# Windowed attention and multiplicative FFN on one core: Q and K of the first batch loaded in thirds, w1 and w2 in quarters, two row blocks of w3 by SP in fp32, and a new order of the opening

## The chip, the core and the metric

The kernel runs on one core of a Trainium2 chip. The core has five engines with a queue each, worked off in order: PE (TensorE, matmuls), DVE (VectorE), ACT (ScalarE), POOL (GpSimd) and SP (SyncE), which here only issues transfers. 16 DMA engines move the data; POOL and SP (and once ACT) issue the transfers. The time is device microseconds (us) of one execution; lower is better.

## The reference

```python
# q, k, v: (8, 8, 576, 64) fp32 (batch, head, position, dim)
scores = (q @ k.T) / 8            # kept where 0 <= row - col < 64, else -1e9
attn   = softmax(scores)
x      = (attn @ v) as (8*576, 512) rows    # heads side by side
h      = ((x @ w1) * (x @ w2)) @ w3         # w1, w2: 512x1024, w3: 1024x1024
out    = h @ w_out                          # w_out: 1024x512, out (4608, 512) fp32
```

## The kernel before, in words

Everything is computed in fp16 with fp32 sums. Because nothing stands between w3 and w_out, the kernel first folds them on the chip into one matrix `wc_sb` = w3 @ w_out (1024x512). After that each token costs only x @ w1, x @ w2, the product, and one matmul by `wc_sb`.

The work has four kinds, and all of them meet on PE.

- **Fold.** w3 is cut into eight row blocks of 128 rows. `fold_t(fc)` (L469) transposes one block on PE by eight matmuls with the identity `ident16`, and copies the result from PSUM (the accumulators that PE writes) to the tile `w3Ts[fc]` (L476). `fold_mm(fc, c0, c1, cp)` (L478) multiplies it by columns c0 to c1 of w_out and copies the result into `wc_sb` with the engine `cp`.
- **Attention.** A batch has three groups of 192 query rows. `scores(n)` (L272) is 32 small matmuls on group n and leaves two halves, one for each two pairs of heads; `weigh(d)` (L296) takes half d: exp on ACT (L303), then the window mask, either by POOL with `affine_select` (L258, L260) or by DVE as a product with a ready band of ones (L308). `values(d)` multiplies the weights by V and ones (L337 for batches 0 to 2, L353 after), so that the sums of the softmax come out of the same matmuls; then log and exp on ACT (L343, L344) and a product on DVE (L345) give the columns of `xT`, the FFN's input. `transposes(b, which, hh)` (L219) turns loaded Q or K rows by DVE (L225), which `scores` needs. `copy_v` copies halves of V blocks on DVE.
- **FFN.** Tokens go in nine groups of 512. `ffn_ab(g, fc, nf, lo, hi)` (L401) makes nf blocks of 128 of the 1024 hidden columns for tokens lo to hi of group g: matmuls (L417), a copy by ACT (L422), a product by DVE (L423). `ffn_o(g, t)` (L426) multiplies 128 tokens by `wc_sb` (L435) and copies the result out (L437); `store` (L440) sends it away on SP's queue.
- **Filler.** `keep_busy(n)` (L502) is n matmuls of the identity by itself, whose result nobody reads.

PSUM has two pools: `ps_a`, two tiles used by `scores` and `values`, and `ps_f`, four tiles used in turn by the fold, the FFN and the filler. A matmul that needs the next tile of a pool waits until the copy that read its earlier contents is done.

The order of the work on each engine is the order of the calls in the source (L516 on): nothing is reordered. Loads are issued by POOL, with a cast from fp32 to fp16 on the way. At most eight of POOL's loads are outstanding: each takes one of eight semaphores in turn, and waits until the load that had it eight issues ago has landed. `load_qk` (L202) loads Q or K of a batch in four loads by head pairs; `load_w12` (L454) loads halves of w1 or w2, `load_wo` (L459) halves of w_out, `load_w3` (L463) two row blocks of w3. From `tick(24)` (L614) on the order comes from a loop that interleaves attention `tick`s with FFN parts by due times (L622 to L649).

In the opening, POOL first issues the four K loads of batch 0, then makes the identity, issues the four Q loads, half of w_out and two blocks of w3; PE runs 120 filler matmuls, `scores(0)`, 30 more, and then the fold begins. The FFN of group 0 (L575) starts when the fold and all of batch 0's attention are done.

Of the kernel before, what the change touches and what calls it, by code (L numbers as in the profile page):

```python
# [144 lines left out]
def kernel(  # L145
# [25 lines left out]
    EARLY = 2  # L171
# [28 lines left out]
    RUN = [9] * 3 + [2] * (B - 3)  # L200

    def load_qk(b, which, *hhs):  # L202
        src = k if which == "k" else q
        r = RUN[b]
        if (which, b) not in t16s:
            t16s[which, b] = sb.tile([P, 2, TI * D], FP16, name=which + "16", bufs=2)
        t = t16s[which, b]
        if not hhs:
            for j in range(NJ):
                nc.gpsimd.dma_start(  # L210
                    out=t[32 * j:32 * j + 32].rearrange("p hh (i n) -> p (hh i) n", n=r * D),
                    in_=src[b, 2 * j:2 * j + 2].rearrange("hh (i p r) d -> p (hh i) (r d)", p=32, r=r))
        for hh in hhs:
            for i in range(2):
                nc.gpsimd.dma_start(
                    out=t[:, hh, i * r * D:(i + 1) * r * D],
                    in_=src[b, hh:H:2, i * 32 * r:(i + 1) * 32 * r].rearrange("j (p r) d -> j p (r d)", p=32, r=r))

    def transposes(b, which, hh):  # L219

        dst = kTs if which == "k" else qTs
        r = RUN[b]
        if hh == 0:
            dst[b] = sb.tile([P, 2, S, 2], FP16, name=which + "T")
        nc.vector.transpose(  # L225
            dst[b][:, hh].rearrange("q t c -> q (t c)").bitcast(I32).rearrange("q (i p r) -> q i r p", p=32, r=r),
            t16s[which, b][:, hh].bitcast(I32).rearrange("p (i r e) -> p i r e", r=r, e=32))
# [44 lines left out]
    def scores(n, now=True):  # L272
# [19 lines left out]
        weigh(2 * n)  # L292
        if now:
            weigh(2 * n + 1)

    def weigh(d):  # L296
# [9 lines left out]
        if d % 2 == 1 and d < 6 * EARLY:  # L306
# [7 lines left out]
    def values(d):  # L314
# [11 lines left out]
        r = sb.tile([P, 2, 192], FP32, name="r")
        x0 = (b * S + q_base) % RING
        xs = xT[:, j0:j0 + 2, x0:x0 + 192]
        if b < SHORT:
# [15 lines left out]
            nc.vector.tensor_tensor(xs, o, r, ALU.mult)  # L345
            return
        for jj in range(2):
            first = True
            for a in range(2):
# [104 lines left out]
    def load_w12(i, half):  # L454
        cols = slice(half * 512, half * 512 + 512)
# [3 lines left out]
    def load_wo(half):  # L459
        cols = slice(half * 256, half * 256 + 256)  # L460
        nc.gpsimd.dma_start(out=wo16[:, :, cols], in_=moe_w_out[:, cols].rearrange("(e p) m -> p e m", p=P))  # L461

    def load_w3(n):  # L463
        fc = 2 * n
        dst = w3a[:, 2 * fc:2 * fc + 4, :].rearrange("p (f a) n -> p f (a n)", f=2) if n < 2 else \
            xT[:, fc - 4:fc - 2, 2 * S:2 * S + DF]
        nc.gpsimd.dma_start(out=dst, in_=moe_w3[fc * P:fc * P + 2 * P].rearrange("(f p) n -> p f n", p=P))

    def fold_t(fc):  # L469
# [6 lines left out]
        dve_cp(w3Ts[fc], tp)  # L476
# [39 lines left out]
    load_qk(0, "k")  # L516
# [170 lines left out]
```

## Time and profile before

| what | value |
|---|---|
| median of 3 runs | 268.73 us (267.65 to 269.23) |
| profiled execution | 268.59 us, of which 266.8 us span from first to last instruction and 1.79 us around it |
| granted TensorE clock | 0.997 |
| busy ACT / DVE / POOL | 151.4 / 169.7 / 178.7 us |
| bytes: POOL's queue / hardware queues of SP and ACT | 19.41 MB / 9.59 MB |

PE's timeline by stage, from the windows view (stretch, PE busy, PE idle):

| stretch (us) | what PE does | PE busy | idle |
|---|---|---|---|
| 0 to 17.4 | filler, scores(0), waiting for loads | 11.44 | 5.96 |
| 17.4 to 40 | fold, scores(1), scores(2), values(0) to values(5) | 22.20 | 0.40 |
| 40 to 54 | ffn_ab of group 0 | 14.00 | 0 |
| 54 to 73 | batch 1's attention, ffn_o of group 0, start of group 1 | 18.04 | 0.96 |
| 73 to 250 | the loop | 177.00 | 0 |
| 250 to 267 | last FFN parts, last stores | 11.71 | 5.29 |

A line of the timeline gives the start, the time from the first start to the last end, engine, code line, operation, what it writes and reads, the number of instructions, and in brackets how long the engine was idle before and for what. "Busy" on PE counts pipelined matmuls from start to modelled end. DMA rows give the destination and source tile; sizes of POOL's loads are those written (fp16).

### The profile page before, as it was taken

The numbers are of one execution on the slowest core, as the hardware profiler recorded it, in microseconds if no ns is written. First come the engines' busy times: TensorE is split into PE (matmuls) and PEld (weight loads), VectorE is DVE, ScalarE is ACT, GpSimd is POOL, SyncE is SP. The second block draws the span as 40 slices with busy tenths as digits, with TensorE's granted clock in tenths as the row PEclk, the third lists the DMA queues.
The fourth block names the chain that finished last, engine by engine and source line by source line (L and its number), as shares of the span: only waits on it lengthen the run. The fifth ranks groups of instructions, "written<-read, shape, count | busy, mean of one in ns | idle before, by whom it ended". The sixth has DMA issues, their size and how long they took to land.

```text
span 266.8 us, 6600 instructions
## 1 busy us (share of the span) xinstructions
PE 254.4 (95%) x2608; PEld 149.7 (56%) x2608; DVE 169.7 (64%) x260; ACT 151.4 (57%) x261; POOL 178.7 (67%) x243
## 2 busy tenths in 40 slices
PE   3979999998999999999999999999999999999992
PEld 3968654445886445545556984545455445444441
DVE  6644454978775675986687567668786565564531
ACT  1037474367656577758874855777498748342300
POOL 7979826679879999999898739687766345005000
PEclk9999999999999999999999999999999999999998
DMA  5999999999999999899999765998540040012013
GB/s 81 170 207 186 189 207 201 131 181 138 149 106 62 131 206 77 61 165 162 62 106 180 102 43 64 202 105 57 99 96 4 7 150 6 0 53 108 0 57 109
DMA packets 75380, 29.45 MB, mean 110 GB/s; under 512 B 62369, under 2 KB 69793, under 8 KB 75345
## 3 DMA queue, kind: packets, MB, share of 16 engines
q0 software_dynamic: 69920, 19.41, 74.9%
q1 hardware_dynamic: 5280, 9.46, 10.0%
q8 instruction: 21, 0.34, 0.6%
q14 instruction: 15, 0.11, 0.2%
q10 hardware_dynamic: 144, 0.13, 0.1%
HBM read 38.80 MB, written 9.44 MB: 181 GB/s over the span
## 4 chain that ended last, share of the span: by engine, by line
PE 87%; DMA 4%; POOL 2%; DVE 2%; ACT 2%; issue 1%; POOLq 0%; DVEq 0%
PE f_ps L417 48%; PE f_ps L435 22%; PE a_ps L353 5%; PE a_ps L286 4%; PE f_ps L481 4%; DMA ab<-in_moe_w_dram 4%; PE a_ps L337 3%; ACT pt L303 1%; PE f_ps L474 1%; POOL q L210 1%; POOL k L210 1%; DVE xT L345 1%; DVE kT L225 1%; POOL ab L461 0%; DVE pt L308 0%
## 5 line engine op out<-in xcount | busy, mean ns | idle before, releaser
L417 PE MATMUL f_ps<-xT,w_sb 128*128 128x512 f16 (+1 forms) x704 | 131.5, 341 | 0.0
L417 PEld LDWEIGHTS <-w_sb 128*128 128x128 f16 x704 | 66.3, 98 | 50.7 <-issue 0.2
L423 DVE TENSOR_TENSOR ab<-f_ps,a_sb 128x512 f16<-128x512 f32 x72 | 49.6, 689 | 33.0 <-PE f_ps L417 31.2
L303 ACT ACTIVATE pt<-a_ps 128x1024 f16<-128x1024 f32 (+1 forms) x48 | 44.5, 953 | 45.4 <-PE a_ps L286 45.4
L258 POOL TENSOR_SCALAR_AFFINE_SELECT pt<-pt 128x1024 f16<-128x1024 f16 (+2 forms) x56 | 46.1, 824 | 30.6 <-ACT pt L303 30.5
L435 PE MATMUL f_ps<-wc_sb,ab 128*128 128x512 f16 (+1 forms) x296 | 66.4, 374 | 0.0
L422 ACT COPY a_sb<-f_ps 128x512 f32<-128x512 f32 x72 | 41.8, 581 | 36.9 <-PE f_ps L417 36.4
L260 POOL TENSOR_SCALAR_AFFINE_SELECT pt<-pt 128x1024 f16<-128x1024 f16 (+2 forms) x56 | 46.5, 831 | 3.9
L435 PEld LDWEIGHTS <-ab 128*128 128x128 f16 x296 | 27.3, 98 | 28.8
L238 POOL DMA_DIRECT2D v<-in_v_dram x40 | 34.0, 860 | 1.0 <-issue 0.4
L362 DVE TENSOR_TENSOR xT<-a_ps,r 64x384 f16<-64x384 f32 x30 | 16.5, 550 | 22.0 <-ACT r L361 22.0
L437 DVE COPY t2k<-f_ps 128x512 f32<-128x512 f32 (+1 forms) x35 | 23.7, 679 | 8.4 <-PE f_ps L435 7.9
L210 POOL DMA_DIRECT2D q<-in_q_dram x32 | 19.7, 621 | 11.8 <-DMA w_sb<-in_moe_w_dram 8.3
L210 POOL DMA_DIRECT2D k<-in_k_dram x32 | 20.1, 634 | 1.6 <-POOLq L671 1.0
L353 PEld LDWEIGHTS <-v 128*128 128x128 f16 x240 | 15.1, 98 | 6.4
L345 DVE TENSOR_TENSOR xT<-a_ps,r 128x384 f16<-128x384 f32 x18 | 10.0, 553 | 13.0 <-ACT r L344 13.0
L359 ACT ACTIVATE ln_s<-a_ps 64x384 f32<-64x384 f32 x30 | 14.6, 487 | 5.8 <-PE a_ps L353 5.0
L353 PE MATMUL a_ps<-pt,v 128*128 128x128 f16 x240 | 17.2, 215 | 0.0
L363 DVE TENSOR_TENSOR xT<-a_ps,r 64x384 f16<-64x384 f32 x30 | 16.8, 561 | 0.4
L286 PEld LDWEIGHTS <-kT 32*128 32x128 f16 x768 | 10.9, 92 | 9.6 <-issue 9.3
L361 ACT ACTIVATE r<-ln_s 128x384 f32<-128x384 f32 x30 | 15.7, 523 | 1.0
L225 DVE STREAM_TRANSPOSE qT<-q 128x576 int32<-128x576 int32 x16 | 14.7, 928 | 1.6 <-DMA q<-in_q_dram 1.6
(44 smaller groups left out, 184.9 us busy)
## 6 DMA issues: line engine op xcount, KB each, us to landing
out_dram<-t2k SPq DMA_DIRECT2D x35, 256.0 KB
k<-in_k_dram POOLq DMA_DIRECT2D x32, 144.0 KB, 6.3
q<-in_q_dram POOLq DMA_DIRECT2D x32, 144.0 KB, 5.8
v<-in_v_dram POOLq DMA_DIRECT2D x32, 128.0 KB, 5.0
w_sb<-in_moe_w_dram POOLq DMA_DIRECT2D x4, 512.0 KB, 9.7
ab<-in_moe_w_out_dram POOLq DMA_DIRECT2D x2, 512.0 KB, 9.5
ab<-in_moe_w_dram POOLq DMA_DIRECT2D x2, 512.0 KB, 9.4
xT<-in_moe_w_dram POOLq DMA_DIRECT2D x2, 512.0 KB, 10.4
```

Source lines behind the costliest of these rows:

```text
L210: nc.gpsimd.dma_start(out=t[32 * j:32 * j + 32].rearrange("p hh (i n) -> p (hh i) n", n=r * D), in_=src[b, 2 * j:2 * j + 2].rearrange("hh ...
L238: nc.gpsimd.dma_start(out=vh[lo:P, c], in_=v[b, :, s0:s0 + P - lo, :].rearrange("h s d -> s h d"))
L258: nc.gpsimd.affine_select(out=sl, in_=sl, pattern=pat, compare_op=ALU.is_ge, fill=0.0, base=off, channel_multiplier=-1)
L260: nc.gpsimd.affine_select(out=sl, in_=sl, pattern=[[-s, m] for s, m in pat], compare_op=ALU.is_ge, fill=0.0, base=63 - off, channel_multip ...
L286: nc.tensor.matmul(s_ps[j // 2][:, j % 2, o0:o0 + m], kT[part, a, k0:k0 + P, c], qT[part, a, q0:q0 + m, c], start=(c == 0), stop=(c == 1), ...
L303: nc.scalar.activation(pt[:, :, :, 0:w], s_ps, AF.Exp, bias=-SHIFT, scale=scale)
L353: nc.tensor.matmul(o_ps[:, jj, o0:o0 + n], v16[:, si * 2 + bi, j0 + jj, a * D:a * D + P], pt[:, jj, a, c0:c0 + n], start=first, stop=(bi = ...
L417: nc.tensor.matmul(d[:, f * n + c0:f * n + c1], w[:, dc, (fc + f) * P:(fc + f + 1) * P], xT[:, dc, xc:xc + c1 - c0], start=first, stop=(dc ...
L422: act_cp(a_sb[:, 0:nf * n], a_ps[:, 0:nf * n])
L423: nc.vector.tensor_tensor(ab[:, fc:fc + nf, lo:hi], b_ps[:, 0:nf * n].rearrange("p (f n) -> p f n", f=nf), a_sb[:, 0:nf * n].rearrange("p ...
L435: nc.tensor.matmul(o_ps[:, 0:c1 - c0], ab[:, fc, t * P:t * P + P], wc_sb[:, fc, c0:c1], start=(fc == 0), stop=(fc == 7))
L437: cp(o_sb[:, c0:c1], o_ps[:, 0:c1 - c0])
```

## The change

The loads of batch 0's Q and K become twelve: for K and Q, for the even and the odd heads (hh), for each third i of the positions (192 rows, 96 KB in fp16); `transposes` gets a form for one third. w1 and w2 come in quarters of 256 columns. Row blocks 0 and 1 of w3 are loaded by SP as they are, 512 KB of fp32 each, into the space of `w2_sb` (which w2's loads fill later), and cast to fp16 in halves of 512 columns by ACT (block 0) and DVE (block 1). `scores` no longer calls `weigh`, and `values` is split into its matmuls and `norm` (log, exp, product), so that each can be placed by itself; which engine masks is given at each call. The order of the calls from the start to the first `ffn_ab` of group 1 is new. After `tick(24)` nothing changes. The diff, cut to its core:

```diff
-    RUN = [9] * 3 + [2] * (B - 3)
+    RUN = [6] + [9] * 2 + [2] * (B - 3)
...
+    def third(b, which, hh, i):
+        r = RUN[b]
+        src = k if which == "k" else q
+        return src[b, hh:H:2, i * 32 * r:(i + 1) * 32 * r].rearrange("j (p r) d -> j p (r d)", p=32, r=r)
+
+    def load_rows(fc, queue):
+        queue.dma_start(out=w2_sb.rearrange("p a n -> p (a n)").bitcast(FP32)[:, fc * DF:fc * DF + DF],
+                        in_=moe_w3[fc * P:fc * P + P])
+
+    def cast_rows(fc, x, cp):
+        n = DF // 2
+        cp(w3a[:, 2 * fc + x, :],
+           w2_sb.rearrange("p a n -> p (a n)").bitcast(FP32)[:, fc * DF + x * n:fc * DF + x * n + n])
+
...
+    def load_third(b, which, hh, i):
+        n = RUN[b] * D
+        nc.gpsimd.dma_start(out=t16_of(b, which)[:, hh, i * n:(i + 1) * n], in_=third(b, which, hh, i))
+
+    def transposes(b, which, hh, *i):
...
+        part = slice(i[0], i[0] + 1) if i else slice(0, TI // r)
         nc.vector.transpose(
-            dst[b][:, hh].rearrange("q t c -> q (t c)").bitcast(I32).rearrange("q (i p r) -> q i r p", p=32, r=r),
-            t16s[which, b][:, hh].bitcast(I32).rearrange("p (i r e) -> p i r e", r=r, e=32))
+            dst[b][:, hh].rearrange("q t c -> q (t c)").bitcast(I32).rearrange("q (i p r) -> q i r p", p=32, r=r)[:, part],
+            t16s[which, b][:, hh].bitcast(I32).rearrange("p (i r e) -> p i r e", r=r, e=32)[:, part])
 
...
-    def scores(n, now=True):
+    def scores(n):
...
-        weigh(2 * n)
-        if now:
-            weigh(2 * n + 1)
-
-    def weigh(d):
+
+    def weigh(d, engine=nc.gpsimd):
...
-        if d % 2 == 1 and d < 6 * EARLY:
+        if engine is nc.vector:
...
-            o, total = (o_ps[:, e, 0:384].rearrange("p (j n) -> p j n", j=2) for e in range(2))
-            nc.scalar.activation(y, total, AF.Ln)
-            nc.scalar.activation(r, y, AF.Exp, scale=-1.0)
-            nc.vector.tensor_tensor(xs, o, r, ALU.mult)
...
+    def norm(d):
+        b, r = divmod(d, 6)
...
+        if b < SHORT:
+            o, total = (o_ps[:, e, 0:384].rearrange("p (j n) -> p j n", j=2) for e in range(2))
+            nc.scalar.activation(y, total, AF.Ln)
+            nc.scalar.activation(r, y, AF.Exp, scale=-1.0)
+            nc.vector.tensor_tensor(xs, o, r, ALU.mult)
...
-    def load_w12(i, half):
+    def load_w12(i, c0, c1):
...
-    def fold_t(fc):
+    def fold_t(fc, cp):
...
-        dve_cp(w3Ts[fc], tp)
+        cp(w3Ts[fc], tp)
...
-    load_qk(0, "k")
+    load_rows(1, nc.sync)
+    load_third(0, 'k', 1, 0)
+    ones_of(0, nc.vector)
+    transposes(0, 'k', 1, 0)
+    load_third(0, 'k', 0, 0)
     make_identity(nc, ident16)
-    load_qk(0, "q")
-    load_wo(0)
-    load_w3(0)
+    load_w3(2, 2)
+    keep_busy(85)
     make_bands()
-    load_w3(1)
-    load_wo(1)
-    load_w3(2)
-    load_v(0, 0, 2, 3)
-    for i in range(2):
-        ones_of(i, nc.vector)
-    for which in "kq":
-        for hh in range(2):
-            transposes(0, which, hh)
-    keep_busy(120)
+    transposes(0, 'k', 0, 0)
+    load_third(0, 'k', 1, 1)
+    load_rows(0, nc.sync)
+    load_third(0, 'q', 0, 0)
+    load_third(0, 'q', 1, 0)
+    load_wo(0, 256)
+    cast_rows(0, 0, act_cp)
+    keep_busy(20)
+    load_wo(256, 512)
+    load_w3(4, 2)
+    load_third(0, 'k', 0, 2)
+    cast_rows(0, 1, act_cp)
+    load_third(0, 'q', 0, 1)
+    transposes(0, 'k', 1, 1)
+    load_v(0, 0)
+    load_third(0, 'k', 0, 1)
+    transposes(0, 'q', 1, 0)
+    keep_busy(20)
+    fold_t(0, act_cp)
+    load_third(0, 'q', 1, 1)
+    load_w3(6, 2)
+    load_v(0, 2)
+    transposes(0, 'q', 0, 0)
+    cast_rows(1, 0, dve_cp)
+    load_third(0, 'q', 0, 2)
+    load_third(0, 'q', 1, 2)
+    fold_t(3, act_cp)
+    keep_busy(25)
     scores(0)
-    keep_busy(30)
-    fold_t(0)
-    fold_t(1)
+    cast_rows(1, 1, dve_cp)
+    load_third(0, 'k', 1, 2)
+    fold_t(2, act_cp)
+    load_v(0, 3)
+    fold_t(1, dve_cp)
+    ones_of(1, nc.gpsimd)
+    fold_mm(0, 0, 256, act_cp)
+    fold_mm(1, 0, 256, dve_cp)
+    weigh(1, nc.vector)
+    load_v(0, 4)
+    load_w12(0, 256, 512)
+    weigh(0, nc.vector)
+    fold_mm(2, 0, 256, dve_cp)
+    fold_mm(2, 256, DM, dve_cp)
+    fold_mm(0, 256, DM, act_cp)
+    transposes(0, 'k', 0, 2)
+    fold_mm(1, 256, DM, act_cp)
+    fold_t(4, act_cp)
+    fold_mm(3, 0, 256, act_cp)
+    load_v(0, 5)
+    fold_mm(3, 256, DM, dve_cp)
+    transposes(0, 'q', 1, 1)
+    load_w12(1, 256, 512)
+    transposes(0, 'q', 0, 1)
+    fold_t(5, act_cp)
+    transposes(0, 'k', 0, 1)
+    fold_mm(4, 0, DM, act_cp)
+    load_w12(1, 0, 256)
+    copy_v(0, 1)
     scores(1)
-    load_w3(3)
-    load_v(0, 4, 5)
-    fold_mm(0, 0, 256, act_cp)
-    fold_mm(1, 0, 256, act_cp)
-    fold_t(2)
-    fold_t(3)
-    scores(2)
-    for i in range(2):
-        load_w12(i, 0)
-    fold_mm(2, 0, 256, act_cp)
-    fold_mm(3, 0, 256, act_cp)
-    fold_mm(0, 256, DM, act_cp)
-    fold_mm(1, 256, DM, act_cp)
-    fold_t(4)
-    fold_t(5)
-    fold_mm(2, 256, DM, act_cp)
-    fold_mm(3, 256, DM, act_cp)
-    copy_v(0, 1)
-    fold_mm(4, 0, DM, act_cp)
+    weigh(2, nc.vector)
+    transposes(0, 'q', 1, 2)
+    weigh(3, nc.gpsimd)
+    load_w12(0, 0, 256)
+    fold_t(7, dve_cp)
+    fold_mm(5, 256, DM, dve_cp)
+    load_w12(0, 512, 768)
     values(0)
+    load_w12(1, 512, 768)
+    norm(0)
+    transposes(0, 'k', 1, 2)
+    fold_mm(5, 0, 256, dve_cp)
     values(1)
-    fold_t(6)
-    fold_mm(5, 0, DM, act_cp)
+    load_qk(1, 'k')
+    load_qk(1, 'q')
+    norm(1)
+    fold_t(6, act_cp)
+    transposes(0, 'q', 0, 2)
+    fold_mm(7, 0, DM, dve_cp)
     values(2)
     values(3)
+    load_w12(0, 768, 1024)
+    norm(2)
+    norm(3)
+    load_w12(1, 768, 1024)
     copy_v(0, 4)
-    fold_t(7)
-    fold_mm(6, 0, DM, act_cp)
+    fold_mm(6, 0, DM, dve_cp)
+    load_v(1, 4)
+    scores(2)
+    weigh(4, nc.vector)
+    ffn_ab(0, 2, 2, 0, 256)
+    weigh(5, nc.vector)
     values(4)
+    norm(4)
+    load_qk(2, 'k')
+    keep_sums(0)
+    ffn_ab(0, 0, 2, 0, 256)
     values(5)
-    fold_mm(7, 0, DM, act_cp)
-    for i in range(2):
-        load_w12(i, 1)
-    load_qk(1, "k")
-    load_qk(1, "q")
-    load_v(1, 0, 2, 3, 4, 5)
-    for n in range(3):
-        keep_sums(n)
-    for fc in range(8):
-        ffn_ab(0, fc)
-        if 2 <= fc < 6:
-            transposes(1, "kkqq"[fc - 2], fc % 2)
-    load_qk(2, "k")
-    load_qk(2, "q")
+    load_v(1, 2)
+    norm(5)
+    load_v(2, 3)
+    transposes(1, 'k', 0)
+    ffn_ab(0, 4, 2, 0, 256)
+    load_v(1, 0)
+    ffn_ab(0, 0, 2, 256, 512)
+    ffn_ab(0, 2, 2, 256, 512)
+    transposes(1, 'q', 1)
+    load_qk(2, 'q')
+    transposes(1, 'k', 1)
+    keep_sums(1)
+    transposes(1, 'q', 0)
+    ffn_ab(0, 4, 2, 256, 512)
+    ffn_ab(0, 6)
+    ffn_ab(0, 7)
+    transposes(2, 'k', 0)
+    load_v(1, 3)
+    load_v(1, 5)
+    scores(3)
+    weigh(6, nc.gpsimd)
+    weigh(7, nc.vector)
+    ffn_o(0, 0, dve_cp)
+    scores(4)
+    weigh(8, nc.gpsimd)
     copy_v(1, 1)
+    ffn_o(0, 1, dve_cp)
+    weigh(9, nc.vector)
+    store()
+    load_v(2, 0)
+    scores(5)
+    transposes(2, 'k', 1)
+    weigh(10, nc.vector)
+    load_v(2, 4)
+    ffn_o(0, 2, dve_cp)
+    weigh(11, nc.gpsimd)
+    values(6)
+    norm(6)
+    values(7)
+    norm(7)
+    store()
+    load_qk(3, 'k')
+    ffn_o(0, 3, act_cp)
+    transposes(2, 'q', 1)
     copy_v(1, 4)
-    scores(3)
-    ffn_o(0, 0)
+    values(8)
     store()
-    scores(4)
-    load_v(2, 0, 2, 3)
-    ffn_o(0, 1)
-    store()
-    scores(5)
-    transposes(2, "k", 0)
-    ffn_o(0, 2, act_cp)
-    store()
-    values(6)
-    transposes(2, "k", 1)
-    values(7)
-    load_v(2, 4, 5)
-    ffn_o(0, 3)
-    store()
-    values(8)
-    transposes(2, "q", 0)
     values(9)
-    load_qk(3, "k")
-    load_qk(3, "q")
+    keep_sums(2)
+    norm(8)
+    norm(9)
+    load_v(2, 5)
     ffn_ab(1, 0, 2, 0, 256)
+    keep_sums(3)
+    transposes(2, 'q', 0)
+    values(11)
     values(10)
-    transposes(2, "q", 1)
+    norm(10)
+    norm(11)
     ffn_ab(1, 2, 2, 0, 256)
-    values(11)
-    for n in range(3, 6):
-        keep_sums(n)
+    load_v(2, 2)
+    keep_sums(4)
+    load_qk(3, 'q')
+    keep_sums(5)
     U0 = 24
     ffn_ab(1, 4, 2, 0, 256)
```

62 lines of the change are left out of this document (31 added, 31 removed).

## The prediction

> **What bounds the kernel now.** I read the page first: the busy shares, the strip of 40 slices, the chain's summary.
>
> ```profile
> PE 254.4 (95%) x2608; PEld 149.7 (56%) x2608; DVE 169.7 (64%) x260; ACT 151.4 (57%) x261; POOL 178.7 (67%) x243
> PE   3979999998999999999999999999999999999992
> DMA  5999999999999999899999765998540040012013
> PE 87%; DMA 4%; POOL 2%; DVE 2%; ACT 2%; issue 1%; POOLq 0%; DVEq 0%
> ```
>
> PE is the bound, and is short of full only in the first slices and the last. The windows view says where: no idle from 73 to 250 us. The last 5 us of idle are the closing stores, which the change doesn't touch. So the change is worth what it moves the first matmul of `tick(24)`, now at 72.87; from there the code is the same and PE has no gap to fill or lose. The chain and PE's timeline show what comes before.
>
> ```profile
> 7.51 9.87 DMA ab<-in_moe_w_dram
> 17.38 0.05 issue
> 17.43 1.07 PE f_ps L474 x16
> ```
>
> ```profile
> 4.57 5.61 PE L506 MATMUL f_ps<-ident 128*128 128x128 f16 x59 [4.57 <-POOL ident masks.py:199]
> ...
> 14.51 0.41 PE L286 MATMUL a_ps<-qT,kT 32*128 32x128 f16 x24 [0.70 <-DVE qT L225]
> 14.85 1.85 PE L506 MATMUL f_ps<-ident 128*128 128x128 f16 x30
> 17.43 1.07 PE L474 MATMUL f_ps<-ident,ab 128*128 128x128 f16 x16 [0.73 <-DMA ab<-in_moe_w_dram]
> ```
>
> The fold starts at 17.43, released by w3's first load, issued at 7.51 behind all of Q and K. Until then PE has done nothing useful but `scores(0)`. "Busy" hides this: L506 is the filler. From there to `ffn_ab(0, 0)` at 39.94 the matmuls run nearly without a break (22.5 us, 0.3 of it waits). Batch 1 has waits of its own:
>
> ```profile
> 61.38 0.89 PE L337 MATMUL a_ps<-pt,v 128*64 128x128 f16 x32
> 62.20 1.90 PE L435 MATMUL f_ps<-wc_sb,ab 128*128 128x512 f16 x8
> 64.20 0.64 PE L337 MATMUL a_ps<-pt,v 128*64 128x128 f16 x16
> 65.61 0.64 PE L337 MATMUL a_ps<-pt,v 128*64 128x128 f16 x16 [0.78 <-DVE xT L345]
> ```
>
> **The change on PE, step by step.** *Start.* Two K loads (0.81 + 0.55) stand ahead of the identity instead of four (2.44): 1.1 earlier, so filler from 3.5. Of the filler, 43 matmuls come 107 ns apart (12 to 13 per us in the windows), the rest 56 ns (22 per us); the first phase lasted 4.57 us. So 85 take 4.57 + 42 x 0.056 = 6.9, and 20 + 20 another 2.2: `fold_t(0)` at 12.6. Then two `fold_t` (16 matmuls, 0.9), 25 fillers (1.4), `scores(0)` (0.45), done at 15.35. The old kernel, at its 17.43, had `scores(0)` behind it but no `fold_t`; the new one has two more done (0.9), so is 17.43 - (15.35 - 0.9) = 3.0 ahead.
>
> The Trainium skill, "TensorE: Matmul & The Clock Gate", Part 1, says that the slow phase ends with a free-running window of 3.4 us, so its length depends on where the first matmul falls. The trace's 4.57 agrees. As an estimate by that page, 3.4 instead would end the fillers 0.6 earlier, and 6.8 1.1 later.
>
> *Fold to FFN.* The same matmuls, in another order. From 15.35: two `fold_t` 0.9, eight halves of `fold_mm` at 0.92 (32 matmuls of 256 took 3.67 at 22.50), two `fold_t` 0.9, `fold_mm(4)` 1.8, `scores(1)` 0.6, and so on to `scores(2)`: 20.5. One wait: `scores(2)` needs both `ps_a` tiles, held by `values(2)` and `values(3)` until `norm` is through: log 0.49 and exp 0.52 twice on ACT, then the product 0.56 on DVE, 2.65 after `values(2)` ends, against 2.3 of matmuls there: 0.35. So the first `ffn_ab` at 36.2.
>
> *FFN of group 0.* Six calls of 16 matmuls of 256 at 1.85 (the row at 66.18, less the overlap), two of 1.74 and `values(4)`, `values(5)` between them, 1.0: 15.6. Cutting six calls costs 6 x 0.11 = 0.66 on PE. Next DVE: from 36.2 it has eight products (0.69), two masks (0.77), two norms (0.56) and five transposes of batches 1 and 2 (1.21 each in batch 1): 14.2 us of work in 15.6. By the order given, three transposes stand together ahead of the product of `ffn_ab(0, 4, hi)`, which ends at 51.45; `ffn_ab(0, 7)` wants its PSUM tile at 50.9. I take 0.55 of wait. `scores(3)` at 52.3, against 53.96: 1.65 ahead.
>
> *Batch 1.* Old: 18.91 from there to `tick(24)`, with 17.7 of matmuls and 1.2 of waits, the two lines above among them: `values(9)` waited for a product that stood behind a transpose on DVE. In the new order `norm(6)` and `norm(7)` follow directly, and the transpose comes after them: 1.0 + 1.6 after `values(6)` ends, against 0.5 + 1.83 + 0.5 until `values(9)`. I leave 0.3 for `scores(5)`, which still waits for exp. `tick(24)` at 70.3: 2.6 ahead, and **266.0** against the profiled 268.59 (the median is 268.73, 0.14 more).
>
> **What must be there in time.** The DMA engines work in order of issue and are full from 3 us on. Their service by the landing records: 512 KB of w in 2.6 us whether in rows of 512 B, 1 or 2 KB (w_out 2.61, w3 2.67, w1 2.5); Q and K of batch 0 1.04 per 144 KB, of batch 1 0.72; V about 1.0 per 128 KB. So a third, 96 KB, costs 0.69 early and 0.5 later, a quarter of w1 1.27. Twelve thirds come to what eight loads did, 8.3. The two blocks by SP replace one load of 2.67; no row shows such a load, so: at least 1.4 each (256 packets of 2 KB at 87 ns over 16 engines, as stores took), at most 2.0 (stores of 256 KB ran at 260 GB/s). I take 1.3 to 1.4, the price of the load replaced.
>
> Adding up from 3.2: both blocks and blocks 2, 3 landed by 9.8 (needed 12.6; ACT's two casts, 0.6 each like L482, come between); first thirds 11.9, transposed by 12.7 (`scores(0)`: 14.9); w_out 14.5 and 17.1 (16.25 and 19.0); blocks 4, 5 19.7 (21.75); last thirds of `scores(1)` 23.1, transposed 24 to 25.6 (26.3); blocks 6, 7 25.7 (26.9); V block 2 26.7, copied 27.3 (`values(0)`: 28.3); w1 and w2 quarters 33.5, 34.8 and 36.1, 38.7 (36.2, 38.6, 40.9); K of batch 1 41.6 (42.6); last quarters 47.1 (48.3). So everything is in time, by 1.0 to 2.8 us, and **1.0 is the cover**: a lateness L of the feed costs about L - 1.
>
> The Trainium skill, "DMA: Bandwidth & Descriptors", section "Issuing engines are not separate DMA queues", says that SP's loads run on the same 16 engines as POOL's and interleave. The trace has the two kinds side by side only at 58 and 59 us, too little to tell. By the rule SP's two blocks take the 2.7 counted above; were they free beside POOL's, every landing would be 2.7 earlier and the cover 3.7.
>
> POOL issues 52 loads to `scores(3)`, and the ninth waits for the first to land, as the old Q loads of batch 1 did (34.67 after a landing at 34.38). With eight small loads outstanding (8 x 0.5 = 4 us of transfer) the engines still don't run dry. New on POOL are `ones_of(1)`, about 2.6 (0.33 for 256 columns, linearly to 3072), and one mask (`weigh(3)`, 2.2) where it had three (7.2). The quarters behind `weigh(3)` wait until 31.4 for it, when 3.4 us of transfers are still queued. DVE's new work, the casts of block 1 (0.4 to 0.7 each), twelve short transposes (1.13 / 3 and up; I take 0.4) and two more masks, falls before 30 us, where DVE idles over half of the time.
>
> **Rivals.**
> 1. *The feed is late; the slower end.* If a third costs what a whole early load did (1.04), twelve cost 4.2 more; with SP's blocks at 2.0 each, L = 5.6, and PE waits 4.6 from `values(0)` on, behind V block 2: 270.6. For it: early loads were dear. Against: half blocks of V (64 KB) cost 0.44 to 0.6, so small loads aren't charged whole, and packets of 512 B kept the rate. It equals the old time at L = 3.6, and is slower by 0.5% (270.0) from L = 5.0. In between, L from 2 to 5: 267 to 270.
> 2. *Given back on DVE.* Transposes on DVE stand ahead of FFN products from 42.6 to 51. If they start 1.5 late (K of batch 1, or ACT's share), PE waits for PSUM: 267.5.
> 3. *More.* Early transfers were sparse (115 to 175 GB/s until 12 us, 200 later); SP's packets may fill that. With none of the waits of 0.35, 0.55 and 0.3, 264.8.
>
> **How the numbers follow.** Forecast, cover holds (265.3 to 266.9): 0.50. Partly lost, rivals 1 and 2, up to 270: 0.28. Slower, rival 1 beyond L = 5: 0.12. Rival 3, below 265.3: 0.10. Measurement tells about 0.5%, 1.3 us. Faster by more than that (below 267.3): 0.50 + 0.10 + 0.06 = 0.66; slower (above 270): 0.12; the same: 0.22. The range, 264.8 to 270.0, leaves out the slower case and a part of rival 3.
>
> **What would show it.** Fillers from 3.5; `fold_t(0)` at 12.6 without a wait for ACT's cast; `scores(0)` at 14.9 without one for DVE; no wait of PE for DMA at L474, L481 or L417; first `ffn_ab` at 36.2; `scores(3)` at 52.3; `tick(24)` at 70.3; then no gap to 250. I am wrong if PE waits at L337 for V, at the transposes of blocks 6, 7 for their load, or at w1's last quarter, or if POOL, late from the opening, holds masks back after 73 (it is over 90% busy from 80 to 127 us).

## The result, and the profile after

The changed kernel takes **271.66 us** in the median of 18 runs (269.72 to 273.92), the old one 268.43 on the same chip (267.65 to 269.43): a ratio of **1.0114**, 95% interval 1.0088 to 1.0140. The forecast was 266.0, with a range to 270.0; it is wrong in sign. One of the 18 (273.92), like two runs of a1 and one of a5 (379.4) below, was in a slow state and is left out of its ratio. The profiled execution took 272.53 us with a span of 270.7.

The page, in the lines that answer to those of before: the busy shares, the strips, the summary of the chain.

```profile
PE 254.6 (94%) x2664; PEld 154.4 (57%) x2664; DVE 171.5 (63%) x273; ACT 155.5 (57%) x262; POOL 182.8 (68%) x245
PE   4989899797899999999999999999999999999991
PEclk9999999999999999999999999999999999999999
DMA  6999999999999799899999693997650040012022
PE 73%; DMA 16%; POOL 6%; DVE 2%; issue 1%; POOLq 0%; DVEq 0%
```

PE has as much work as before and the full clock. What changed is the chain: DMA went from 4% to 16% of it, POOL from 2% to 6%. In order of time the chain's long pieces are transfers up to 61 us:

```profile
10.01 9.77 DMA ab<-in_moe_w_out_dram
20.06 9.97 DMA v<-in_v_dram
35.60 2.17 POOL w_sb L480 x3
37.77 7.78 DMA k<-in_k_dram
46.58 6.61 DMA w_sb<-in_moe_w_dram
53.47 7.98 DMA v<-in_v_dram
```

Each piece begins where a load was issued and ends where it landed: the opening runs at the pace of the feed. PE's timeline shows what that cost. The lines are those on which the forecast set a time, and those with a wait in brackets.

```profile
3.71 8.58 PE L529 MATMUL f_ps<-ident 128*128 128x128 f16 x125 [3.71 <-POOL ident masks.py:199]
12.13 1.06 PE L497 MATMUL f_ps<-ident,ab 128*128 128x128 f16 x16
15.49 0.53 PE L301 MATMUL a_ps<-qT,kT 32*128 32x128 f16 x32 [0.91 <-DVE qT L240]
17.17 5.45 PE L504 MATMUL f_ps<-ab,w3T 128*128 128x256 f16 x48 [0.15 <-DMA ab<-in_moe_w_out_dram]
30.40 0.43 PE L343 MATMUL a_ps<-pt,v 128*64 128x64 f16 x12 [0.46 <-DVE v L259]
35.65 0.64 PE L343 MATMUL a_ps<-pt,v 128*64 128x128 f16 x16 [0.53 <-POOL pt L275]
38.62 1.92 PE L441 MATMUL f_ps<-xT,w_sb 128*128 128x256 f16 x16
49.32 3.64 PE L441 MATMUL f_ps<-xT,w_sb 128*128 128x256 f16 x28 [1.26 <-DVE ab L447]
55.93 0.53 PE L301 MATMUL a_ps<-qT,kT 32*128 32x128 f16 x32
68.65 1.08 PE L343 MATMUL a_ps<-pt,v 128*64 128x128 f16 x32 [2.14 <-DVE xT L379]
76.14 0.53 PE L301 MATMUL a_ps<-qT,kT 32*128 32x128 f16 x32
```

The last line is `tick(24)`: 76.14, where the forecast had 70.3 and the old kernel 72.87. The 5.8 that it is later than forecast came in three places: 2.4 up to the first `ffn_ab` (38.62, forecast 36.2), 1.2 in group 0's `ffn_ab` (17.31 long, forecast 16.1), 2.2 in batch 1 (20.21, forecast 18.0). Another 0.7 came behind PE's last matmuls, in the closing stores of this execution.

The waits name DVE and POOL, but two of them go back to the feed. The 1.26 before 49.32: `ffn_ab`'s product stood on DVE behind `transposes(1, 'k', 0)`, which had waited 2.27 for K of batch 1, landed at 47.41. The 2.14 before 68.65: `copy_v(1, 1)` waited on DVE for a V block that landed at 61.45, and the norm of `values(6)` stood behind it.

Which loads were late? The landings (when the last of a load's 16 completion events came) against the forecast:

| load | forecast | landed | late |
|---|---|---|---|
| SP's blocks and blocks 2, 3 of w3 | 9.8 | 11.10 | 1.3 |
| first thirds of K and Q | 11.9 | 14.55 | 2.7 |
| w_out, first half | 14.5 | 17.12 | 2.6 |
| blocks 4, 5 of w3 | 19.7 | 22.30 | 2.6 |
| V block 2 | 26.7 | 30.04 | 3.3 |
| K of batch 1 | 41.6 | 47.41 | 5.8 |
| last quarters of w1, w2 | 47.1 | 53.19 | 6.1 |

Two steps, then: 2.6 by 14 us, which stays until 26, and another 3 between 26 and 47. The experiments ask what made each.

### The profile page after: what moved, and what is told of

Same layout as the page of the kernel before. It is cut to its first block, busy times and chain, and to the rows that moved or that the text cites. A ratio compares the mean times of both kernels' runs of the same rounds, so it can differ in the third digit from the quotient of the medians.

```text
span 270.7 us, 6718 instructions
## 1 busy us (share of the span) xinstructions
PE 254.6 (94%) x2664; PEld 154.4 (57%) x2664; DVE 171.5 (63%) x273; ACT 155.5 (57%) x262; POOL 182.8 (68%) x245
## 4 chain that ended last, share of the span: by engine, by line
PE 73%; DMA 16%; POOL 6%; DVE 2%; issue 1%; POOLq 0%; DVEq 0%
PE f_ps L441 42%; PE f_ps L459 21%; DMA v<-in_v_dram 7%; PE a_ps L355 5%; DMA ab<-in_moe_w_out_dram 4%; PE a_ps L301 4%; DMA k<-in_k_dram 3%; DMA w_sb<-in_moe_w_dram 2%; PE a_ps L343 2%; POOL w_sb L480 2%; POOL k L231 1%; DVE pt L320 1%; DVE t2k L461 1%; POOL q L231 0%; DVE v L257 0%
## 5 line engine op out<-in xcount | busy, mean ns | idle before, releaser
L441 PEld LDWEIGHTS <-w_sb 128*128 128x128 f16 x752 | 70.8, 98 | 47.8 <-issue 1.4
L273 POOL TENSOR_SCALAR_AFFINE_SELECT pt<-pt 128x1024 f16<-128x1024 f16 (+2 forms) x53 | 44.1, 831 | 30.1 <-ACT pt L315 30.1
L275 POOL TENSOR_SCALAR_AFFINE_SELECT pt<-pt 128x1024 f16<-128x1024 f16 (+2 forms) x53 | 43.8, 826 | 3.6
L240 DVE STREAM_TRANSPOSE kT<-k 128x576 int32<-128x576 int32 (+1 forms) x20 | 15.7, 783 | 11.9 <-DMA k<-in_k_dram 11.7
L206 POOL DMA_DIRECT2D q<-in_q_dram x28 | 17.7, 642 | 2.9 <-DMA w_sb<-in_moe_w_dram 2.5
L206 POOL DMA_DIRECT2D k<-in_k_dram x28 | 17.6, 640 | 0.3 <-issue 0.3
L355 PE MATMUL a_ps<-pt,v 128*128 128x128 f16 x240 | 17.2, 215 | 0.0
L240 DVE STREAM_TRANSPOSE qT<-q 128x576 int32<-128x576 int32 (+1 forms) x20 | 15.2, 774 | 2.9 <-DMA q<-in_q_dram 2.8
```

Of the source, the lines that this page charges most:

```text
L206: nc.gpsimd.dma_start(out=t[32 * j:32 * j + 32].rearrange("p hh (i n) -> p (hh i) n", n=r * D), in_=src[b, 2 * j:2 * j + 2].rearrange("hh ...
L240: nc.vector.transpose(dst[b][:, hh].rearrange("q t c -> q (t c)").bitcast(I32).rearrange("q (i p r) -> q i r p", p=32, r=r)[:, part], t16s ...
L273: nc.gpsimd.affine_select(out=sl, in_=sl, pattern=pat, compare_op=ALU.is_ge, fill=0.0, base=off, channel_multiplier=-1)
L275: nc.gpsimd.affine_select(out=sl, in_=sl, pattern=[[-s, m] for s, m in pat], compare_op=ALU.is_ge, fill=0.0, base=63 - off, channel_multip ...
L355: nc.tensor.matmul(o_ps[:, jj, o0:o0 + n], v16[:, si * 2 + bi, j0 + jj, a * D:a * D + P], pt[:, jj, a, c0:c0 + n], start=first, stop=(bi = ...
L441: nc.tensor.matmul(d[:, f * n + c0:f * n + c1], w[:, dc, (fc + f) * P:(fc + f + 1) * P], xT[:, dc, xc:xc + c1 - c0], start=first, stop=(dc ...
```

## The experiments

Each ratio is against the old kernel on the same chip, with its 95% interval; "us" is the ratio less one, times 268.5. The changed kernel stands at +3.1.

| run | what | ratio | us |
|---|---|---|---|
| b5 | old, early Q and K loads in the shape of the thirds | 1.0160 [1.0136, 1.0185] | +4.3 |
| b2 | old, twelve thirds | 1.0153 [1.0134, 1.0171] | +4.1 |
| b3 | old, quarters of w1, w2 | 1.0003 [0.9985, 1.0020] | +0.1 |
| b1 | old, SP's rows | 0.9977 [0.9962, 0.9991] | -0.6 |
| b4 | b1 without 30 fillers | 0.9966 [0.9948, 0.9984] | -0.9 |
| a1 | changed, without SP's rows | 1.0149 [1.0098, 1.0199] | +4.0 |
| a2 | changed, second ones by DVE | 1.0088 [1.0050, 1.0127] | +2.4 |
| a4 | changed, halves of w1, w2 | 1.0088 [1.0066, 1.0110] | +2.4 |
| a5 | changed, ones by DVE and halves | 1.0030 [1.0007, 1.0054] | +0.8 |
| a3 | changed, whole Q and K loads | 1.0102 [1.0060, 1.0144] | +2.7 |
| c1 | changed, all three of these | 0.9987 [0.9968, 1.0006] | -0.3 |
| c2 | c1, calls moved on POOL and DVE | 1.0145 [1.0123, 1.0168] | +3.9 |
| d0 | changed, sixteen small loads | 1.0174 [1.0130, 1.0218] | +4.7 |
| d1 | d0, ones by DVE and halves | 1.0116 [1.0082, 1.0150] | +3.1 |
| d2 | d1, w3's last blocks earlier | 1.0190 [1.0155, 1.0224] | +5.1 |

### The shape of a load (b5, b2)

A load of the old kernel fills 32 partitions with one pair of heads; its outermost dimension is the 32 rows. b5 keeps the number of loads, their bytes and the length of their rows, and changes what is outermost: it takes the even or the odd heads (hh), four heads by 32 rows into all 128 partitions, as a third does. `load_qk` of the old source has this form too:

```diff
-    load_qk(0, "k")
+    load_qk(0, "k", 0, 1)
...
-    load_qk(0, "q")
+    load_qk(0, "q", 0, 1)
```

> The kernel before with batch 0's Q and K in the same number of loads of the same size and the same 1152 B rows, but each over 4 heads of 32 partitions (128 partitions, one run each) instead of 32 partitions with 4 runs: the shape of the thirds alone. Theory E: landings of each load come in groups of four engines and spread over 2 us or more; the last Q load lands 0.5 to 2 later than 12.1, scores(0) with it, and time is 268.5 to 270. Rival N: landings, spread (0.5 to 2) and time (268.2) as before.

272.53 us (271.47 to 273.54), +4.3: the shape alone makes the old kernel as slow as the changed one, or slower. The 16 completion events of each of the first three K loads, old kernel above, b5 below (issue, then the times of the events):

```
 1.49   4.2 4.2 4.3 4.3 4.4 4.4 4.5 4.5 4.6 4.6 4.6 4.7 4.7 4.7 4.8 4.8
 2.29   5.1 5.1 5.2 5.2 5.2 5.3 5.3 5.3 5.3 5.4 5.4 5.4 5.4 5.5 5.5 5.8
 2.84   6.0 6.0 6.0 6.1 6.1 6.1 6.2 6.3 6.5 6.6 6.6 6.7 6.7 6.8 7.2 7.5

 1.43   3.5 3.5 3.5 3.5 3.6 3.6 3.6 3.6 3.6 3.6 3.7 3.8 7.2 7.3 7.3 7.9
 2.36   4.3 4.3 4.3 4.3 4.3 4.4 4.4 4.5 7.4 7.5 7.6 8.1 9.2 9.2 9.3 9.5
 3.07   5.0 5.0 5.1 5.1 7.6 7.7 7.8 8.3 9.4 9.5 9.5 9.7 10.7 10.8 10.9 10.9
```

In the old kernel the engines finish within 0.6 to 1.5 us of each other. In b5 twelve report the first load at once, and the other four, which carry it, 3.7 us later; as the groups of events read, the next load falls to the next four, and every load ends with its four. Q was complete at 15.5 where it was at 12.1, and PE's timeline of b5 has the fold 3.2 later. Part of the rest goes with PE's clock: the two executions with a mean granted clock of 0.996 and 0.997 took 272.13 and 271.47, the four with 0.990 to 0.993 took 272.45 to 273.54.

```profile
16.86 0.42 PE L286 MATMUL a_ps<-qT,kT 32*128 32x128 f16 x24 [1.75 <-DVE qT L225]
20.64 1.07 PE L474 MATMUL f_ps<-ident,ab 128*128 128x128 f16 x16 [1.57 <-DMA ab<-in_moe_w_dram]
```

The Trainium skill states the rule, in "DMA: Bandwidth & Descriptors", section "Why a DMA increments its semaphore by 16 and not by 1": a load is spread over the largest number of engines up to 16 that divides the slowest dimensions of both sides, which for four heads is four. The trace agrees: groups of four. b2 puts the real thirds in:

```diff
+    for hh, i in ((0, 0), (1, 0), (0, 1), (1, 1)):
+        load_third(0, "k", hh, i)
```

> The kernel before with one part of the change: Q and K of batch 0 in twelve thirds (outermost dimension four heads) in the place of its eight loads; nothing else moves. My prediction's own step (twelve thirds take what eight loads take) gives no change, 268.3, with fold_t(0) at 17.4. If what costs is that each load is worked by four of the sixteen engines, as in the run with the shape alone, it gives the same again: landing events in groups of four, fold_t(0) at 20 to 21.5, 272 to 273.2. If each further load is charged besides (0.5 to 1.0 for each of the four more), 274 to 276.

272.86 us (272.07 to 273.93): by the time, the same again. By the landings it is not quite: Q was complete at 16.4 (b5: 15.5), and `fold_t(0)` stood at 21.51 (20.64). The thirds landed 0.90 apart, where I had 0.69; the 144 KB loads of b5 landed 1.09 apart. So the shape is most of the price, and the number of loads adds little that the times can tell.

### SP's rows and the fillers (a1, b1, b4)

a1 takes SP's two loads and the casts out of the changed kernel, and POOL loads blocks 0 and 1 with its cast, ahead of blocks 2 and 3.

```diff
-    load_rows(1, nc.sync)
...
+    load_w3(0, 2)
     load_w3(2, 2)
```

> The changed kernel with row blocks 0 and 1 of w3 loaded by POOL with the cast (512 KB in fp16), just ahead of blocks 2 and 3; no load by SP, no casts on ACT and DVE. Theory F (the feed as a whole is late, through POOL's issue and many small loads between 17 and 40 us): the transfer replaced costs the same 2.7 us, so the Q third that scores(0) needs still lands near 14.5, w1's and w2's last quarters near 53, and the time stays within 0.7 of the changed kernel's 271.7. Rival R (SP's fp32 blocks, which had the DMA engines to themselves from 2.4 to 5.4 us, are what made it late by 2.6): 269.1.

No faster than the changed kernel: +4.0, and the intervals overlap. Without SP's rows `fold_t(3)` waits 2.08 for blocks 2, 3. b1 puts the rows alone into the old kernel, in the place of `load_w3(0)`.

```diff
+    load_rows(1, nc.sync)
+    load_rows(0, nc.sync)
...
-    load_w3(0)
```

> The kernel before with one part of the change alone: row blocks 0 and 1 of w3 by SP in fp32, cast by ACT (block 0) and DVE (block 1); POOL's load of them is left out, all else as before. Theory F: the same bytes of service, only earlier in the order, so Q lands later and w_out as before: 267.9 to 269.0. Rival R: the fold and scores(0) start 2.6 later, 270 to 271.

267.54 us (267.03 to 268.38), -0.6. From 2 to 8 us the engines moved 262 GB/s, in the old kernel 128; the last Q load landed at 12.2, in the old kernel at 12.1. I had priced the two blocks at 2.7, and they landed 1.3 apart, as priced (4.59 and 5.92). The first K load then came 1.8 later than in the old kernel (6.60 against 4.84), but the eight loads of K and Q followed 0.8 apart and not 1.04, and by the last of them nothing of the 2.7 is left. But the fold, ready 0.8 earlier, still stood behind 30 fillers. b4 drops them.

```diff
     scores(0)
-    keep_busy(30)
```

> The kernel before with w3's blocks 0 and 1 by SP in fp32, as in the run of that part alone, and without the 30 filler matmuls between scores(0) and fold_t(0). There the fold waited for the filler only (16.62, no wait), w_out had landed at 14.8 and blocks 2 and 3 at 18.1, and the feed was 2 us ahead. Theory F (time is set by when PE's useful work starts, as long as the feed is ahead): fold 1.7 earlier, 265.8 to 266.6. Rival: the gain is given back at blocks 2 and 3 or at w1 and w2: 267.5.

267.52 us (266.66 to 268.35), no better than b1 by more than the intervals. `fold_t(0)` came 1.56 earlier, at 15.06, and `fold_mm(0)` only 0.32:

```profile
15.06 1.07 PE L483 MATMUL f_ps<-ident,ab 128*128 128x128 f16 x16
16.74 0.63 PE L295 MATMUL a_ps<-qT,kT 32*128 32x128 f16 x30 [0.45 <-ACT pt L312]
18.02 1.92 PE L490 MATMUL f_ps<-ab,w3T 128*128 128x256 f16 x16 [0.65 <-DVE w3T L485]
```

An earlier start of the fold was given back within 3 us, here to ACT's exp and DVE's copy. That is a first sign that the forecast's gain of 3.0 at the start was not to be had as such.

### POOL's ones, and the quarters (a2, a4, b3, a5)

From 17 to 30 us POOL's work in the changed kernel includes this (in brackets what it waited for before):

```profile
17.41 0.74 POOL L490 DMA_DIRECT2D xT<-in_moe_w_dram  x1 [1.90 <-DMA ab<-in_moe_w_out_dram]
20.06 0.92 POOL L253 DMA_DIRECT2D v<-in_v_dram  x1 [1.92 <-DMA ab<-in_moe_w_out_dram]
22.59 0.72 POOL L231 DMA_DIRECT2D q<-in_q_dram  x1 [1.61 <-DMA xT<-in_moe_w_dram]
...
26.85 2.68 POOL L535 MEMSET v<- 128x3072 f16 x1
29.45 0.71 POOL L253 DMA_DIRECT2D v<-in_v_dram  x1
```

Three loads waited for the landing eight issues back, and then 2.68 us went into the ones. a2 lets DVE fill them at the start.

```diff
     ones_of(0, nc.vector)
+    ones_of(1, nc.vector)
...
-    ones_of(1, nc.gpsimd)
```

> The changed kernel with the second memset of ones on DVE right behind the first (4.2 to 7 us, where DVE waits for K), not on POOL at 26.85. Theory F: POOL's 2.7 us between two V loads are gone, and copy_v(0, 1), which took 2.37 beside that memset, takes 0.3; loads from V block 4 on land 1.5 to 2.5 earlier, PE's waits shrink by as much: 269.2 to 270.2. Rival R (SP's blocks) and rival D (the order on DVE from 42 us on): within 0.5 of 271.7.

270.15 us (269.11 to 272.38), +2.4. By itself that can't be told from the +3.1 of the changed kernel, but the profile has both effects. The feed, by windows (the last column is GB/s), old kernel first (with other loads in this stretch), then the changed one, then a2:

```profile
30.00:36.00 6.00, 6.00 (x96) 3.84 (x95) 2.27 (x4) 4.67 (x10) 3.10 (x6) 1.00 1.34 200
```

```profile
30.00:36.00 6.00, 5.07 (x81) 3.47 (x83) 5.05 (x11) 3.73 (x7) 5.93 (x8) 1.00 1.46 119
```

```profile
30.00:36.00 6.00, 5.93 (x92) 3.84 (x91) 4.72 (x11) 4.09 (x8) 5.52 (x7) 1.00 1.76 174
```

And a copy on DVE, which took 2.37 us beside POOL's memset in the changed kernel (first line) and 0.38 in a2:

```profile
27.30 2.37 DVE L257 COPY v<-v 64x512 f16<-64x512 f16 x1
```

```profile
27.45 0.38 DVE L257 COPY v<-v 64x512 f16<-64x512 f16 x1
```

The Trainium skill, "SBUF — State Buffer", section "SBUF: two separate sides", has GpSimd and some of VectorE's operations share a pair of ports that one of them holds for a whole instruction. The trace agrees: the copy ended at 29.67, 0.14 after the memset.

a4 keeps POOL's ones and loads w1 and w2 in halves again:

```diff
-    load_w12(0, 256, 512)
+    load_w12(0, 0, 512)
```

> The changed kernel with w1 and w2 in halves of 512 columns (four loads instead of eight), each where its first quarter stood. Theory F: quarters landed 1.46 us apart where half a half is 1.27, and four slots of POOL are freed; last columns land about 1.5 earlier, but the first ones 1.3 later, at about 37 to 40, near their need at 38.6: 270.2 to 271.5. Rivals R and D: 271.7, or slower by the later first columns.

270.60 us (270.32 to 270.76), +2.4, like a2 not clear of the changed kernel. The quarters had landed 1.46 apart, where I had 1.27. b3 puts the quarters into the old kernel:

> The kernel before with one part of the change: w1 and w2 in eight quarters of 256 columns in the place of four halves. In the changed kernel a quarter took 1.46 to land where I had 1.27, and halves in their place were worth 1.1. If a quarter costs that much by itself, all of w lands 1.0 to 1.5 later than 42.5 here, and since the first FFN products at 39.9 wait for it, 268.8 to 269.8. Rival: quarters cost only where the feed is already late; here w1 and w2 are issued early enough, and the time stays at 268.0 to 268.6.

268.62 us (267.65 to 270.31): nothing in the old order, where the feed is not late. a5 takes both out of the changed kernel and leaves the thirds:

> The changed kernel with its thirds, but the second ones by DVE and w1, w2 in halves (the two edits that were worth 1.5 and 1.1 alone). If the two add up and the thirds' shape still costs about 1 in this order, 269.0 to 269.6, above the 268.1 that the version with whole loads gave. If the shape costs what it costs in the old order (4), nothing like that can be left of it: 270.5 or more. If the thirds are free in this order, 267.8 to 268.4.

269.35 us (268.75 to 271.26), +0.8. This is clear of the changed kernel: POOL's ones and the quarters are worth 2.3 together.

### Whole loads in the new order (a3, c1, c2)

a3 loads Q and K of batch 0 by pairs of heads again, eight loads on 16 engines each, ahead of w_out.

```diff
-    load_third(0, 'k', 1, 0)
...
+    load_pairs(0, 'k', 0, 1)
```

> The changed kernel with Q and K of batch 0 in eight loads by head pairs (144 KB, as the kernel before shapes them) instead of twelve thirds; the short transposes and all else stay. Theory E (a third's source runs over 4 heads outermost, and its 128 rows are worked by 4 of the 16 DMA engines: in the trace the 16 landing events of a third come in groups of four, 2 to 3 us apart): each load's 16 landings lie within 1 us, loads behind no longer wait for the laggards, POOL's slots come free sooner, w's last quarter lands 1.5 to 3 us earlier than 53.2, time 269.0 to 270.5, though scores(0) starts up to 1.5 later than 15.5 because all of Q is ahead of it. Rival N (each load has a fixed price whatever its shape; eight instead of twelve): the same gain, but the spread of landings stays.

271.25 us (269.50 to 273.19), +2.7: in the median a miss. Its six runs fall into two groups: 269.5 to 270.2 at a mean granted clock of 0.993 to 0.994, as expected, and 272.3 to 273.2 at 0.986 to 0.987. The profile is of the second group, with a clock of 0.64 from 16 to 24 us. The landings lost their groups, but POOL's ones now came at 16.36, beside two casts of block 1 on DVE, which took 3.49 us together; PE waited 1.67 for them. In this execution the memset had only found another victim. c1 takes the ones and the quarters out as well.

> The changed kernel with three parts undone together: Q and K of batch 0 in eight loads by head pairs, the second memset of ones on DVE early, w1 and w2 in halves. Theory F with E: the single gains (1.5 for the memset, 1.1 for the halves, 1 to 2.5 for the shape) add up as long as PE waits for the feed: 266.5 to 268.5. Rival D (the order on DVE from 42 us on and in batch 1 holds 2 to 3 us by itself): 268.5 to 270.

268.11 us (267.00 to 269.66), -0.3: the old kernel's time. The milestones, from its PE timeline:

```profile
16.56 0.53 PE L310 MATMUL a_ps<-qT,kT 32*128 32x128 f16 x32 [1.56 <-DVE qT L249]
18.58 5.43 PE L513 MATMUL f_ps<-ab,w3T 128*128 128x256 f16 x48 [0.49 <-DMA ab<-in_moe_w_out_dram]
```

```profile
72.31 0.53 PE L310 MATMUL a_ps<-qT,kT 32*128 32x128 f16 x32
```

`tick(24)` is at 72.31, 0.6 ahead of the old kernel; the forecast had 2.6. `scores(0)` waits 1.56 for Q, whose last load landed at 15.62, and `fold_mm(0)` 0.49 for w_out, which landed at 18.54 behind whole Q and K. c2 tries to win the rest by order: Q's loads ahead of POOL's bands, block 1's casts ahead of Q's transposes, and `copy_v(1, 1)` behind `weigh(10)`.

> As the version with whole loads, ones by DVE and halves (268.1), with three calls moved: Q's loads ahead of POOL's bands, both casts of w3's second block ahead of Q's transposes on DVE, and copy_v(1, 1) behind weigh(10). If DVE's order is what still holds PE (1.6 at scores(0), 0.65 at values(8) for the column product), scores(0) comes 0.5 to 1.0 earlier, the wait before values(8) goes, tick(24) falls from 72.3 to 71.2 to 71.8, and the time is 267.0 to 267.6. If the feed holds it, what is gained at the opening is lost again at w_out and at the first FFN products, as in the run without the 30 fillers, and it is 267.6 to 268.2.

272.48 us (271.35 to 272.98), +3.9: I was wrong on both counts. At the opening nothing moved: Q's loads were issued 2.7 earlier and landed at 15.61 against 15.62, so POOL's order did not set it. And the copy, behind a masking product and a transpose on DVE, made `values(6)` wait:

```profile
65.31 1.20 PE L352 MATMUL a_ps<-pt,v 128*64 128x64 f16 x28 [3.35 <-DVE v L268]
66.45 3.08 PE L468 MATMUL f_ps<-wc_sb,ab 128*128 128x512 f16 x8
```

### Small loads on sixteen engines (d0, d1, d2)

If four engines to a load are the fault, thirds of a better shape should give what the change aims at. d0 loads the first 192 positions of two heads in one load (48 KB, eight of them), the other 384 in another (96 KB), 32 rows outermost.

```diff
+    out=t[32 * j:32 * j + 32, :, 2 * s0:2 * s1],
+    in_=src[0, 2 * j:2 * j + 2, s0:s1].rearrange("hh (p r) d -> p hh (r d)", p=32)
```

> The changed kernel, with the early part of batch 0's Q and K still loaded ahead of the rest, but by loads whose outermost dimension is 32 rows and not four heads: for each pair of heads the first 192 positions of both heads (48 KB, eight loads), and the other 384 positions in one load (96 KB, eight loads), where the twelve thirds stood; DVE transposes the 384 at once. All else as changed. If the four engines to a load are what cost in the thirds, and not their being small and many, the landings lose their groups of four, scores(0) comes at 14.9 to 15.4 (15.49) and w_out at 14.8 to 16 (17.12), and the time falls by 1 to 3 to 268.5 to 270.5, the rest of the lateness (POOL's ones, the quarters) staying. If smallness or the number of loads costs, 16 loads are worse than 12: 272 to 274.

273.95 us (271.00 to 274.29), +4.7: the hope fails, and the time lies on the other side of the expectation. The groups of four are gone and `scores(0)` runs at 15.00, but w_out landed at 18.16. With ones by DVE and halves:

> The same with the second ones by DVE and w1, w2 in halves, worth 1.5 and 1.1 alone in the changed kernel. If the three causes are the shape, POOL's ones and the quarters, this version has the order that the change aims at without them: fold_mm(0) at 16.5 to 17 (18.58 with whole loads), tick(24) at 70.8 to 71.8, 266.3 to 267.5, below both kernels. If the feed's bytes hold the opening whatever their shape, it comes to what whole loads gave, 267.8 to 268.5.

271.14 us (270.68 to 272.93), +3.1, against +0.8 with thirds (a5) and -0.3 with whole loads. `scores(0)` came at 14.55, better than forecast, and this is what it cost on POOL:

```profile
18.58 0.54 POOL L234 DMA_DIRECT2D q<-in_q_dram  x1 [3.02 <-DMA ab<-in_moe_w_out_dram]
20.96 0.54 POOL L234 DMA_DIRECT2D q<-in_q_dram  x1 [1.84 <-DMA ab<-in_moe_w_out_dram]
23.40 1.20 POOL L234 DMA_DIRECT2D q<-in_q_dram  x2 [1.90 <-DMA xT<-in_moe_w_dram]
24.59 0.72 POOL L505 DMA_DIRECT2D xT<-in_moe_w_dram  x1
```

With eight loads outstanding, small ones fill the slots, and the next load waits for w_out to land. Blocks 6 and 7 of w3 could be issued only at 24.59, in c1 at 13.55; they landed at 31.33, and PE waited 1.20 for them. PE had also waited 2.00 for w_out and 1.65 for Q, and the granted clock behind these waits was 0.70 from 32 to 36 us. d2 issues them ahead of the four Q loads.

> The version with 16 small loads on sixteen engines, ones by DVE and halves (271.1), with w3's last two blocks issued ahead of the four later Q loads instead of behind them. In that version POOL waited three times for a slot (3.0, 1.8, 1.9) before the Q loads, w3's last blocks landed at 31.3, and PE waited 1.2 for them and 1.65 for Q. If the limit of eight outstanding loads is what the extra loads cost, w3 lands by 28 and its wait goes, the Q wait stays or grows by 0.5, and the time falls by 0.5 to 1.5 to 269.6 to 270.6. If the bytes hold, one wait is paid for the other: 270.9 to 271.4.

273.59 us (273.28 to 274.78), +5.1, outside both expectations. That wait went, and the one for Q grew from 1.65 to 4.36, by more than I had allowed:

```profile
32.32 1.04 PE L316 MATMUL a_ps<-qT,kT 32*128 32x128 f16 x32 [4.36 <-DVE qT L240]
```

In these two orders the first load to go only chose who waits. That the eight slots, and not the bytes, ration the opening is argued and not shown: d2 met neither expectation.

## Why the prediction was wrong

- *What bounds the kernel, and where a gain is decided.* Right. From 73 us on PE has no gap in either kernel, and its last matmuls moved by 3.27, as `tick(24)` did.
- *The start on PE.* Nearly right: fillers from 3.71 (3.5), `fold_t(0)` at 12.13 (12.6) without a wait for ACT's cast, `scores(0)` at 15.49 (14.9), after 0.91 for Q's transpose on DVE, where I had no wait. The 12.13 has some luck in it: with the same fillers `fold_t(0)` stood at 13.47 in a4.
- *"Twelve thirds come to what eight loads did, 8.3."* **This step failed.** In the old order they cost 4.1 (b2), most of it by their shape (b5): Q was complete at 16.4 and not at 12.1, so twelve thirds came to about 12.6. I had scaled 1.04 by bytes, and held up V's half blocks as proof that small loads aren't charged whole. Those loads have 64 rows outermost, the thirds four heads; the rows that I compared didn't share what decided. In the changed kernel's order the thirds cost about 1.1 (a5 against c1, which differ in the shape of these loads and in their number and place too). That it is less there because large loads between the thirds keep the other engines busy is argued, not shown.
- *SP's blocks at 1.3 to 1.4 each.* Right by their own landings (4.51 and 5.83 in the changed kernel). Charging them to every later landing was too dear: in b1 the loads behind came closer together, and the last Q load landed at 12.2 against 12.1. This was an error on the safe side. (I had also read that the old trace shows SP's and POOL's transfers side by side only at 58 and 59 us; it has them at 64 to 68 us too.)
- *POOL: "the engines still don't run dry", with the ones (2.6) and `weigh(3)` (2.2) covered.* **Failed too.** The size of the memset was right (2.68), the cover wasn't there: 119 GB/s from 30 to 36 us, and the quarter behind `weigh(3)` was issued at 35.55, where I had 31.4. With the quarters it makes 2.3 of the 3.1 (a5), and it took DVE along, which I hadn't thought of.
- *"1.0 is the cover: a lateness L of the feed costs about L - 1."* Nearly right. By the last quarters L was 6.1, which makes 5.1, and `tick(24)` came 5.8 later than forecast.
- *The fold to the first `ffn_ab`: 3.0 ahead, 36.2.* **Failed**, and not to be had even with all three causes gone: c1 is there at 38.70. Its fold starts at 12.54 as forecast, but PE then waits 1.56 for Q, 0.49 for w_out and 0.4 in two smaller places. `fold_mm(0)` began between 17.2 and 18.7 in every version of the changed kernel but a3, for want of w_out in most, where I had 16.25 with w_out landed at 14.5. The 2.5 that are missing in c1 are the gain that I forecast.
- *Rival 1, "the feed is late", 270.6 at a chance of 0.12.* This is what happened, with its size (L of 5.6, measured 6.1), but not for its reasons. Its 4.2 for twelve thirds is what b2 shows (Q 4.3 later), yet eight loads of the same shape are 3.4 later too (b5), so it isn't mainly a price for each load; and it wasn't SP's blocks. That its size came out in the changed kernel, where POOL's ones and the quarters made the larger part, is luck. Rival 2, DVE's transposes ahead of the FFN products, happened too (1.26), as a result of the late K. Of rival 3, SP's packets did fill the sparse early transfers (b1).

So the loss is accounted for: from +3.1, taking out POOL's ones and the quarters is worth 2.3, and whole loads for the thirds another 1.1; what is left, -0.3, can't be told from the old kernel. PE's clock is a smaller part: the changed kernel's four runs in the ratio with a mean granted clock of 0.992 to 0.994 took 272.0 to 273.7, and the median of the 13 with 0.996 and more is 271.1, still 2.7 above the old kernel. Not settled is whether the new order could gain with a better feed: each way I tried to feed it earlier (c2, d1, d2) was a loss. Also a2 and a4 don't separate the ones from the quarters. The best versions are b4 and b1, the old kernel with SP's rows (b4 without 30 fillers too), at 0.9966 and 0.9977 of its time.

## What to carry to other kernels

Look at the outermost dimension of a load before its bytes: events that land in groups of four say that four engines carry it, and a price may only be taken from a row with the same outermost dimension. Cutting loads smaller buys an early first piece with slots and issue time, and where eight may be outstanding the loads behind pay. A forecast that rests on a cover of 1 us needs the feed priced by loads of its own kind; otherwise the late case deserves more than 0.12.

## What the hardware showed unexpectedly

A wait of PE can cost more than its length, since the granted clock sometimes falls behind it. In c2 the wait of 3.35 was followed by eight matmuls of 512 in 3.08 us where they take 1.90, and the windows (granted clock third from the end) show why:

```profile
64.00:66.00 2.00, 0.69 (x21) 0.69 (x22) 1.92 (x3) 0.09 (x1) 2.00 (x3) 0.86 0.05 3
66.00:68.00 2.00, 2.00 (x18) 0.96 (x15) 0.64 (x2) 1.82 (x4) 2.00 (x4) 0.50 1.11 122
```

In d2, behind 4.36, the clock is 0.50 as well. In d0 the clock was 0.79 from 16 to 24 us around a wait of 1.68, and 48 matmuls of `fold_mm` took 7.08 us instead of 5.45. In the profiled execution of the changed kernel the waits, 2.14 at most, left it at 1.00, and so did 2.00 in d1 at the place of d0's 1.68. So the length of one wait doesn't decide it in these traces, and what does is open. The same kernel can go either way, as the two groups of a3 show.

SP's 1 MB of fp32 rows cost the last Q load nothing: the old kernel moves 128 GB/s from 2 to 8 us, b1 with the rows 262, and the last Q load lands at 12.1 and 12.2.
